# Sharing query copies between two engines and pairing score groups in a sparse attention with an expert layer on one core

## The chip, the core and the metric

The kernel runs on one core of a Trainium2 chip. The metric is the device time of one execution in microseconds (us), measured on the chip; less is better. Before the change it is 208.15 us, the median of three runs from 207.64 to 208.67. Separately, one execution was profiled. Its span, from the first instruction to the last, is 205.6 us.

## What is computed

For 4 batches, 8 heads, 768 positions and 64 elements per head, each query attends to two kinds of keys: the keys within 15 positions of its own, and 24 summary keys, each the maximum over a block of 32 keys, with the mean over the block's values. The result, 3072 rows of 512, goes through two dense layers with a gate between them.

```python
k_sum = k.reshape(B, H, nb, block, D).max(axis=3)       # block = 32, nb = 24
v_sum = v.reshape(B, H, nb, block, D).mean(axis=3)
scores_l = scale * np.matmul(q, k.transpose(0, 1, 3, 2))  # kept where |i - j| < 16
scores_s = scale * np.einsum('bhsd,bhnd->bhsn', q, k_sum) + np.log(block)
...
a = softmax of both together; x = np.matmul(a, [v, v_sum])
h = x @ w_in                                             # 512 -> 2048
g = h * (1.0 / (1.0 + np.exp(-1.702 * h)))
out = g @ w_out                                          # 2048 -> 512
```

## The kernel before, in words

**Tiles.** The 768 positions are cut in two halves of 384, the 8 heads in 4 pairs. Of a pair and a half, one *score group* (`scores`, lines 573 to 579) is 12 small matrix products (64 queries by 128 keys: own window, halo and block summaries) into one PSUM buffer of the pool `psb`, tag `big`, which has two buffers, and then one exponential on ScalarE into `a_sb`. `mask` (581 to 584) multiplies `a_sb` by a 0/1 mask on VectorE. `values` (586 to 608) multiplies two pairs' `a_sb` with the values into two banks of the pool `pmm`, tag `mm` (four buffers), and divides by the sums on VectorE (`norm`: a reciprocal and a product each). `tx` (616 to 622) transposes the result on TensorE and VectorE copies it into `xT`. `tq` (547 to 550) transposes one pair's queries on TensorE; VectorE copies them into `qT`.

**The two units.** Batch 0 is treated in two units of 384 rows each. A unit's dense layers are an input stage (`ff_in`, 640) and an output stage: 12 steps of `ff_out` (848 to 859), each with four products of 128x128 by 512, and every fourth part of a row block ended by a copy to SBUF on ScalarE (`osb`) and a write to memory from SP's queue. Attention work for what comes later is laid between these steps by a table that says after which step what is issued:

- unit 0's output stage runs `beside0` (1018 to 1031) with `plan0` (1008): the second half of batch 0. `q_late` (402 to 409) transposes a pair's late queries on TensorE into a PSUM buffer (pairs 0, 1 and 3 into `big`, pair 2 into `mm`) and an engine copies them into `qT`; then come score groups, masks, values and transposes. A `big` buffer goes from a late query to a score group when the copy has read it.
- unit 1's output stage runs `beside(1, step)` (1033 to 1051) with `plan1` (1010 to 1012): all of batch 1's attention. In the table `s02` is the score group of half 0 and pair 2, `m02` its mask, `v00` the values of half 0 and pairs 0 and 1, `x00` the transposes after it, `t2` the query transposes of pair 2, `g` the load of the gate function's table on ScalarE.

Later batches (loop at line 1100) have no halves: both are done together, with another table, `plan`, in which score groups stand in pairs.

**What sets the order.** Every engine's instructions are kept in the order in which the Python code issues them (class `_Ordered`, lines 18 to 32). A helper records them, so the profile gives line 28 for all, and its rows are told apart by tile names: `ps_q` late queries, `ps_t` other transposes, `ps_s` scores, `ps_av` values, `ps_x` transposed results, `po` output products, `ph` input products, `ps_vs` block sums of the values.

**Loads.** GpSimd's queue issues the loads of keys, values and queries (`load_batch`, 231 to 241; for batch 2 after step 2 of unit 1's output stage, line 1094). SP's queue issues the output writes, the key transposes for the next batch (`xk`, 552; after steps 9 and 11, lines 1095 and 1096), the query transposes (`xq`, 559) and the copies within the values (`value_rows`, 1053 to 1058). The block sums (`vsum`, 265 to 281) are 48 products that read a batch's values in the order of their 12 loads; for batch 2 they stand in the input stage after unit 1 (line 1124).

Of the kernel before, what the change touches and what calls it, by code (L numbers as in the profile page):

```python
# [35 lines left out]
def kernel(  # L36
# [28 lines left out]
    dve = _Ordered(tc, nc.vector)  # L65
    act = _Ordered(tc, nc.scalar)
# [187 lines left out]
    def copy(eng, out, in_):  # L254
        if eng is act:
            act.activation(out=out, in_=in_, func=ACT.Copy)
        elif eng == "dve_alone":

            dve.tensor_reduce(out=out, in_=in_.unsqueeze(len(in_.shape)), axis=AX.X, op=ALU.max)
        else:  # L260
            eng.tensor_copy(out=out, in_=in_)
# [96 lines left out]
    def turn_plain(ps, src):  # L358

        for r in range(JH):  # L360
            for h in range(2):
                pe.transpose(out=ps[h * 64:h * 64 + 64, r * 128:r * 128 + 128], in_=src[:, h, r],
                             identity=ident)
# [38 lines left out]
    def q_late(p, eng):  # L402
        if p != 2:
            ps = psb.tile([128, 2048], BF16, name="ps_q", tag="big")
        else:
            ps = pmm.tile([128, 1024], BF16, name="ps_q", tag="mm")
        turn_plain(ps[:, 0:HALF], qb2["late"][:, 2 * p:2 * p + 2])
        copy(eng, qT[p][0][:, HALF:S].rearrange("p (c r) -> p c r", r=JH),
             ps[:, 0:HALF].rearrange("p (r c) -> p c r", r=JH))
# [163 lines left out]
    def scores(b, half, p):  # L573
        a = a_sb[half, p] = attp.tile([128, 2, TH, QT], BF16, name="a_sb", tag="a_sb")
        big = psb.tile([128, 1024], F32, name="ps_s", tag="big")
        score_tiles(big, p, b % 2, half)
        act.activation(out=a.rearrange("p h t c -> p h (t c)"),
                       in_=big.rearrange("p (h c) -> p h c", h=2)[:, :, 0:HALF],
                       func=ACT.Exp, scale=scale)

    def mask(half, p):
        a = a_sb[half, p]
        dve.tensor_mul(a, a, mk[:, half * TH:(half + 1) * TH, :].unsqueeze(1)
                       .to_broadcast([128, 2, TH, QT]))

    def values(b, half, g):

        if b == 1:
            banks = [pmm.tile([128, 512], F32, name="ps_av", tag="mm") for i in range(2)]
        else:  # L590
            ps = psb.tile([128, 1024], F32, name="ps_av", tag="big")
            banks = [ps[:, i * 512:i * 512 + 512] for i in range(2)]
        pvs = []
        for i in range(2):
            p = 2 * g + i
            a = a_sb[half, p]
            pv = banks[i][:, 0:390].rearrange("p (h j c) -> p h j c", h=2, j=JH)
            pvs.append(pv)
            for hh in range(2):
                for j in range(JH):  # L600
                    for e in range(2):
                        t = 2 * j + e
                        pe.matmul(out=pv[e * 64:e * 64 + 64, hh, j, :], lhsT=a[:, hh, t, :],
                                  rhs=vw[b % 2][:, half * TH + t, p + hh * NP if b else 2 * p + hh, 0:D + 1],
                                  start=True, stop=True, skip_group_check=True)
        x2[g] = attp.tile([128, 2, JH, 2, D], F16, name="x2", tag="x2", bufs=4)
        for i in range(2):
            norm(x2[g][:, :, :, i].rearrange("p h j d -> p j h d") if b else x2[g][:, i], pvs[i])
# [7 lines left out]
    def tx(half, g):  # L616
        ps = psb.tile([128, 2, HALF], F16, name="ps_x", tag="big")
        for i in range(2):
            for j in range(JH):
                pe.transpose(out=ps[:, i, j * 128:(j + 1) * 128],  # L620
                             in_=x2[g][:, i, j].rearrange("p h d -> p (h d)"), identity=ident16)
        dve.tensor_copy(out=xTT[half][g], in_=ps)
# [243 lines left out]
    def gelu_soon():  # L866

        act.activation(out=gate[:, 1:2], in_=gate[:, 0:1], func=ACT.Gelu_apprx_sigmoid)
# [130 lines left out]
    for p in range(NP):  # L999
# [7 lines left out]

    plan0 = {1: ["q0", "q1", "q2"], 2: ["q3", "s0", "s1"], 4: ["s2", "s3"], 6: ["v0", "v1"], 8: ["x0"], 9: ["x1"]}

    plan1 = {-1: ["s00", "s01"], 1: ["t2", "m00", "m01"], 2: ["t3", "s02"], 3: ["s03", "m02"], 4: ["m03", "s10"],  # L1010
             5: ["s11", "m10"], 6: ["v00", "m11", "s12", "s13"], 7: ["v01", "g"], 8: ["m12", "m13"],
             9: ["x00", "x01", "v10"], 10: ["v11"], 11: ["x10"]}

    plan = {-1: ["s00", "s01"], 2: ["m00", "m01"], 3: ["s02", "s03"], 5: ["m02", "m03", "s10", "s11"],
# [3 lines left out]
    def beside0(slot):  # L1018
        for what in plan0.get(slot, ()):
            i = int(what[1])  # L1020
            if what[0] == "q":
                q_late(i, dve)
            elif what[0] == "s":
                scores(0, 1, i)
                mask(1, i)
                if i == NP - 1:
                    gelu_soon()
            elif what[0] == "v":
                values(0, 1, i)
            else:  # L1030
                tx(1, i)
# [37 lines left out]
    ws = keep.tile([128, 4, NT // 2, N1], F16, name="ws")  # L1069
    exp_soon()  # L1070
    beside0(-1)
    for i, (ms, part) in enumerate((ms, part) for part in range(4) for ms in range(JH)):
        ff_out(0, ms, part)
        beside0(i)
        if i in (10, 11):
            w_sum(i - 10, 0)
            w_sum(i - 10, 1)
# [22 lines left out]
    for b in range(1, B - 1):  # L1100
# [32 lines left out]
        i = 0  # L1133
# [98 lines left out]
```

## Time and profile before

| | |
|---|---|
| Median of three runs | 208.15 us (207.64 to 208.67) |
| Span of the profiled execution | 205.6 us |
| TensorE busy | 198.5 us, 2364 products |
| VectorE, ScalarE, GpSimd busy | 139.9, 123.7, 93.5 us |
| Unit 0's output stage | about 31 to 46 us of the span |
| Unit 1's output stage | about 59 to 76 us of the span |
| Moved by DMA | 27.74 MB, mean 135 GB/s |

The profiled execution has no time of its own beside its span; the three runs lie 2.0 to 3.1 us above that span. In the profile PE is TensorE's matrix products, PEld its weight loads, DVE VectorE, ACT ScalarE, POOL GpSimd and SP the queue of SyncE. A row of a timeline gives start, length, engine, operation, what is written from what, the count, and in brackets the engine's idle time before it with what ended it. A row of the chain of waits gives start, length and what the chain went through. Of a load, the profile gives the start of its issue and the time from there to its landing.

### The profile page before, as it was taken

Reading aid. Unit: us, or ns where it says so; the run is one execution under the profiler, and the core shown is the slowest. Engines: PE = TensorE matmul, PEld = TensorE weight load, DVE = VectorE, ACT = ScalarE, POOL = GpSimd, SP = SyncE. Lnnn points to the kernel's source line nnn. Section 1 sums busy time; section 2 is a strip of 40 time slices with the busy share of each in tenths; the row PEclk is TensorE's granted clock in tenths of the full one; section 3 lists DMA queues with packets and bytes.
Section 4 is the critical chain, followed back from the end, with each engine's and each line's share of the span. In section 5 each row is a group of like instructions: output and inputs, shape, how many; then the busy total and the mean of one; then the engine's idle time right before and its main releaser. Section 6 shows DMA issues by size and latency. Waiting matters only on the chain.

```text
span 205.6 us, 5854 instructions
## 1 busy us (share of the span) xinstructions
PE 198.5 (97%) x2364; PEld 138.1 (67%) x2364; DVE 139.9 (68%) x388; ACT 123.7 (60%) x237; POOL 93.5 (45%) x145
## 2 busy tenths in 40 slices
PE   7889999999999999999999999999999999999992
PEld 7658564556754566565888875566888865668882
DVE  4767795594856793898757789896769546758221
ACT  2374975728885716677772446778670577983220
POOL 7976289645899585000977036000000019990000
PEclk9999999999999999999999999999999999999999
DMA  5999999999999999999999989999023640000223
GB/s 59 153 158 198 207 212 207 204 156 233 124 145 153 177 170 135 163 145 141 139 180 158 164 162 136 130 248 154 0 105 86 149 126 3 0 0 3 102 102 105
DMA packets 97131, 27.74 MB, mean 135 GB/s; under 512 B 86720, under 2 KB 94160, under 8 KB 97104
## 3 DMA queue, kind: packets, MB, share of 16 engines
q0 software_dynamic: 71472, 13.64, 90.7%
q1 hardware_dynamic: 25632, 13.74, 32.3%
q8 instruction: 18, 0.29, 0.7%
q14 instruction: 9, 0.07, 0.1%
HBM read 27.26 MB, written 6.29 MB: 163 GB/s over the span
## 4 chain that ended last, share of the span: by engine, by line
PE 90%; DMA 4%; POOL 3%; issue 1%; DVE 1%; ACT 0%; POOLq 0%; DVEq 0%
PE ph L28 33%; PE poA L28 16%; PE po L28 11%; PE poB L28 8%; PE ps_av L28 4%; DMA v0n<-in_v_dram 4%; PE poC L28 4%; PE phA L28 4%; PE ps_s L28 3%; PE ps_t L28 1%; POOL kb L28 1%; PE ps_x L28 1%; PE phB L28 1%; PE phC L28 1%; PE phE L28 1%; PE ps_vs L28 1%
## 5 line engine op out<-in xcount | busy, mean ns | idle before, releaser
L28 PE MATMUL ph<-xT,w_in_sb 128*128 128x384 f16 x416 | 70.2, 326 | 0.1
L28 PEld LDWEIGHTS <-w_in_sb 128*128 128x128 f16 x452 | 43.7, 98 | 27.8 <-issue 0.2
L28 ACT ACTIVATE gT<-ph 128x384 f16<-128x384 f32 x104 | 49.8, 491 | 18.5 <-PE ph L28 18.2
L28 PEld LDWEIGHTS <-gT 128*128 128x128 f16 x312 | 28.8, 98 | 11.0
L28 ACT ACTIVATE a_sb<-ps_s 128x768 bf16<-128x768 f32 (+1 forms) x32 | 25.0, 826 | 12.7 <-PE ps_s L28 12.7
L28 PEld LDWEIGHTS <-gs 128*128 128x128 f16 x288 | 27.7, 98 | 3.4
L28 POOL DMA_DIRECT2D vw<-in_v_dram x36 | 24.5, 694 | 12.0 <-DMA kb<-in_k_dram 6.3
L28 POOL TENSOR_TENSOR gs<-gT 128x384 f16<-128x384 f16 x9 | 8.2, 909 | 42.4 <-ACT gT L28 42.4
L28 PE MATMUL po<-w_out_sb,gT 128*128 128x512 f16 x96 | 23.6, 380 | 0.0
L28 DVE TENSOR_TENSOR a_sb<-a_sb,mk 128x768 bf16<-128x768 bf16 x28 | 14.9, 555 | 6.5 <-ACT a_sb L28 5.9
L28 PE MATMUL poA<-ws,gs 128*128 128x256 f16 x144 | 18.7, 273 | 0.0
L28 DVE TENSOR_TENSOR x<-ps_av,rc 128x384 f16<-128x384 f32 x32 | 17.8, 558 | 1.1
L28 DVE TENSOR_TENSOR gs<-gT 128x384 f16<-128x384 f16 (+1 forms) x34 | 13.4, 393 | 7.2 <-ACT gT L28 6.9
L28 POOL DMA_DIRECT2D qb<-in_q_dram x18 | 16.6, 936 | 1.9 <-DMA w_in_sb<-in_moe_w_in_dram 1.2
L28 POOL DMA_DIRECT2D kb<-in_k_dram x16 | 15.3, 970 | 1.2 <-POOLq L1216 0.8
L28 PEld LDWEIGHTS <-kx 64*128 64x128 bf16 (+1 forms) x372 | 9.4, 95 | 6.8 <-issue 4.4
L28 DVE TENSOR_REDUCE ks<-kx 128x24 bf16<-128x768 bf16 x12 | 11.4, 948 | 3.4 <-ACT kx L28 3.2
L28 ACT ACT_TABLE_LOAD x10 | 12.8, 1283 | 1.0 <-PEq L1216 0.8
L28 ACT ACTIVATE osb<-poA 128x256 f32<-128x256 f32 x9 | 3.5, 384 | 15.8 <-PE poA L28 15.8
L28 ACT ACTIVATE s<-poA 128x256 f32<-128x256 f32 x11 | 4.2, 385 | 11.2 <-PE poA L28 11.2
L28 PEld LDWEIGHTS <-a_sb 128*64 128x64 bf16 (+2 forms) x400 | 7.8, 108 | 2.8 <-issue 1.3
L28 PE MATMUL poA<-w_out_sb,gT 128*128 128x256 f16 x72 | 9.4, 273 | 0.0
(113 smaller groups left out, 281.4 us busy)
## 6 DMA issues: line engine op xcount, KB each, us to landing
out_dram<-osb SPq DMA_DIRECT2D x23, 256.0 KB, 3.7
kb<-in_k_dram POOLq DMA_DIRECT2D x16, 192.0 KB, 6.9
qb<-in_q_dram POOLq DMA_DIRECT2D x14, 192.0 KB, 9.2
vw<-in_v_dram POOLq DMA_DIRECT2D x36, 64.0 KB, 5.7
w_out_sb<-in_moe_w_out_dram POOLq DMA_DIRECT2D x4, 512.0 KB, 13.0
w_in_sb<-in_moe_w_in_dram POOLq DMA_DIRECT2D x3, 512.0 KB, 12.7
vw<-vs SPq DMA_DIRECT2D x6, 198.0 KB, 7.1
v0n<-in_v_dram POOLq DMA_DIRECT2D x4, 192.0 KB, 7.9
```

The lines of the kernel that those rows point to most:

```text
L28: r = f(*a, **kw)
```

## The change

In `beside0`, the late query copies of pairs 1 and 3 go to ScalarE instead of VectorE. In `plan1`, half 0's score groups 2 and 3 are both issued after step 3 (before: after steps 2 and 3), half 1's groups 0 and 1 both after step 5 (before: 4 and 5), and half 1's groups 2 and 3 after step 7, behind `v01`, instead of after step 6, behind `v00`. The masks `m02` and `m10` move a step later with them. The number of instructions stays the same on TensorE, GpSimd and SP; VectorE has two fewer, ScalarE two more.

```diff
@@ plan1 @@
-    plan1 = {-1: ["s00", "s01"], 1: ["t2", "m00", "m01"], 2: ["t3", "s02"], 3: ["s03", "m02"], 4: ["m03", "s10"],
-             5: ["s11", "m10"], 6: ["v00", "m11", "s12", "s13"], 7: ["v01", "g"], 8: ["m12", "m13"],
+    plan1 = {-1: ["s00", "s01"], 1: ["t2", "m00", "m01"], 2: ["t3"], 3: ["s02", "s03"], 4: ["m02", "m03"],
+             5: ["s10", "s11"], 6: ["v00", "m10", "m11"], 7: ["v01", "s12", "s13", "g"], 8: ["m12", "m13"],
              9: ["x00", "x01", "v10"], 10: ["v11"], 11: ["x10"]}
@@ beside0 @@
             if what[0] == "q":
-                q_late(i, dve)
+                q_late(i, act if i % 2 else dve)
```

## The prediction

> **What bounds the kernel now.** I read the page first, for which engine is full and at what clock.
>
> ```profile
> span 205.6 us, 5854 instructions
> PE 198.5 (97%) x2364; PEld 138.1 (67%) x2364; DVE 139.9 (68%) x388; ACT 123.7 (60%) x237; POOL 93.5 (45%) x145
> PEclk9999999999999999999999999999999999999999
> DMA  5999999999999999999999989999023640000223
> PE 90%; DMA 4%; POOL 3%; issue 1%; DVE 1%; ACT 0%; POOLq 0%; DVEq 0%
> ```
>
> TensorE is busy for 97% of the span at the full clock, and the chain that ended last is 90% TensorE. So a change can only gain by giving TensorE fewer or cheaper instructions or by closing one of its few gaps. The DMA row is the second thing to see: 9 in nearly every slice up to two thirds of the span. Loads may be as late as TensorE is, and then TensorE time that is saved is waited away at the next load. The list of TensorE's own waits is next. This one of its rows lies in the region of the change:
>
> ```profile
> PE ps_s L28 <- DVE qT L28: 0.4, 1, 0.4
> ```
>
> The times of the runs (207.64, 208.15, 208.67) lie 2.0 to 3.1 us above the profiled span of 205.6. I work out differences within the span and add them to the median, 208.15. The three runs are 0.5% apart from end to end, and I take 0.5%, or 1.04 us, as what a measurement can tell from no change.
>
> **Edit 1: the late query copies 1 and 3 go to ScalarE.** From the timelines of the first unit's output stage and the list of groups by shape:
>
> ```profile
> 33.32 2.15 DVE L28 COPY qT<-ps_q 128x384 bf16<-128x384 bf16 x4 [1.75 <-PE ps_q L28]
> 34.51 0.36 PE L28 MATMUL ps_q<-wide,qb 128*64 128x128 bf16 x6
> 35.52 0.35 PE L28 MATMUL ps_s<-qT,kx 64*128 64x64 bf16 x12 [0.37 <-DVE qT L28]
> L28 DVE COPY qT<-ps_q x8: 548/552/558, 8.8 to 34.9; 128x384 bf16<-128x384 bf16 x8
> L28 ACT ACTIVATE xT<-ps_x 128x384 f16<-128x384 f16 x3 | 1.3, 491 | 0.5 <-PE ps_x L28 0.5
> L28 ACT ACTIVATE qT<-ps_k x3: 810/810/818, 5.9 to 12.2; 128x768 bf16<-128x768 bf16 x3
> 35.25 1.51 ACT L28 ACTIVATE a_sb<-ps_s 128x768 bf16<-128x768 f32 x2 [1.95 <-PE ps_s L28]
> ```
>
> The gap of 0.37 us stands ahead of the second score group, which takes over the PSUM buffer of query group 3 and so waits for the fourth copy. That copy could not have started much earlier on any engine: its six transposes ended at 34.51 + 0.36 = 34.87, and the copy ran from 33.32 + 2.15 - 0.55 = 34.92. Sharing the copies therefore shortens no queue that matters. It only exchanges 0.552 us on VectorE for a ScalarE copy. The trace has none of this exact copy. The same size on ScalarE is the copy of three x tiles, 491 ns: a gain of 0.06 us. The same kind of write (with a stride, into the query and key tile) at twice the size is 810 ns: a loss of 0.26, surely too far, since half of its elements are there. Those are the two ends; I take the one of the same size. Query copy 3 now stands ahead of the first exponentials on ScalarE, which begin at about 35.4 instead of 35.25 and end near 36.95; the scores that reuse their buffers come after 37.6, so that delay is covered.
>
> **Edit 2: the score groups in pairs.** The chain of waits, in order of time, in the second unit's output stage:
>
> ```profile
> 61.20 0.09 issue
> 61.29 0.49 PE ps_t L28 x6
> 61.78 0.86 PE po L28 x4
> 62.65 0.34 PE ps_t L28 x6
> 62.98 0.28 PE ps_s L28 x12
> 63.26 0.97 PE po L28 x4
> ...
> 68.48 0.46 PE ps_s L28 x24
> 68.94 0.97 PE po L28 x4
> ```
>
> Four output products after transposes take 0.86 us, after a score group 0.97. A lone group of 12 score products takes 0.28, a pair 0.46. So a lone group costs 0.28 + 0.11 = 0.39, two cost 0.78, and a pair costs 0.46 + 0.11 = 0.57. Each pairing saves 0.21 us. The change makes two pairs (steps 3 and 5) of four lone groups, and the third pair only moves from behind one block of value products to behind the next. TensorE's work falls by **0.42 us**, all of it before step 6 ends.
>
> What could take this back inside the stage? I count TensorE's new order from 62.98: products 0.86 to 63.84, pair to 64.30, products 0.97 and 0.86 to 66.13, pair to 66.59, products to 67.56, values 0.50, products to 69.03, values to 69.53, pair to 69.99, eight products to 71.82, where before they ended at 72.24.
>
> ```profile
> 63.36 0.55 DVE L28 COPY qT<-ps_t 128x768 bf16<-128x768 bf16 x1
> 68.81 1.51 ACT L28 ACTIVATE a_sb<-ps_s 128x768 bf16<-128x768 f32 x2 [0.94 <-PE ps_s L28]
> 70.20 0.60 ACT L28 ACTIVATE osb<-po 128x512 f32<-128x512 f32 x1
> ```
>
> The fourth group needs the query copy that ends at 63.91 and starts at about 64.02: covered by 0.1. ScalarE now copies the first output block (0.60, from about 63.9) and then does two exponentials (1.51) until about 65.95; the second pair takes their two buffers at 66.13 and 66.31, covered by 0.36. If it weren't, the price would be the missing part alone. The masks that move to steps 4 and 6 stay behind their exponentials, and VectorE has them done by 66.5 against 69.0. VectorE's last run of masks, copies and divisions ends where it does now, so the last block of values may find its buffer 0.1 late. Where something is late next, it is a load.
>
> **Where the gain meets the loads.** Edit 1 first. The second block of query transposes at 61.29 came 0.09 after the products ended, and it reads the last query load of the batch:
>
> ```profile
> L28 POOL DMA_DIRECT2D qb<-in_q_dram x1: 1031/1031/1031, 55.4 to 55.4; - x1
> DMA to landing us min/median/max: 5.8/5.8/5.8
> ```
>
> Landing is 55.4 + 5.8 = 61.2, just there. GpSimd issues this load, its queue does not look at TensorE's progress, and so the start at 61.29 stays where it is. The 0.06 of edit 1 is waited away; I count 0.
>
> Edit 2 next. The block sums of the next batch read its value loads, the last one in their last eight products of 48:
>
> ```profile
> L28 POOL DMA_DIRECT2D vw<-in_v_dram x1: 697/697/697, 75.2 to 75.2; - x1
> DMA to landing us min/median/max: 6.7/6.7/6.7
> 81.65 0.60 PE L28 MATMUL ps_vs<-vw,E 64*32 64x128 bf16 x48
> L28 PE MATMUL ps_vs<-vw,E x48: 213/216/227, 81.6 to 82.0; 64*32 64x128 bf16 x48
> ```
>
> The load lands at 75.2 + 6.7 = 81.9. The last of the 48 products starts at 82.0, the first of the last eight under 0.1 before. So the margin is about 0.05 us. These loads are on GpSimd's queue too, and what holds them up are the landings of earlier loads, not TensorE. If the last one lands where it did, all but 0.05 of the 0.42 us is waited at this place. A second barrier of the same kind follows: the query transposes are issued at 88.0, land 9.6 later at 97.6, and the scores that read them start at 97.89.
>
> ```profile
> L28 SPq DMA_TRANSPOSE qT<-qb x1: 4917/4917/4917, 88.0 to 88.0; - x1
> DMA to landing us min/median/max: 9.6/9.6/9.6
> 97.89 0.41 PEld L28 LDWEIGHTS <-kx 64*128 64x128 bf16 x24 [0.32 <-issue]
> ```
>
> Even a gain that survived the first would be cut to about 0.3 here unless this transfer came earlier as well. The sum: 0 - 0.42 + 0.37 = **-0.05 us**, no change that can be measured.
>
> **The rivals.** *The gain stays.* The output write and key transposes on SP's queue come earlier (next rival); if that clears them out of the loads' way, the last value load and the query transposes land earlier. Then the most is 0.42 + 0.06 = 0.48, and 207.7. For it: the transfers' total is the same. Against it: two barriers must both move.
>
> *The value loads come later* (the other sign). The output copy of the second block now has its products done at 69.03 and is not behind two late exponentials any more; it ends at about 69.7 instead of 70.8. SP's queue is in order, so its write and the key transposes behind it are issued 1.1 us earlier:
>
> ```profile
> 64.94 6.23 SPq L28 DMA_DIRECT2D out_dram<-osb  x2
> 71.34 3.22 SPq L28 DMA_TRANSPOSE kx<-kb  x2
> 76.51 0.34 SPq L28 DMA_DIRECT2D out_dram<-osb  x1
> ...
> q0 software_dynamic: 2381, 0.30, 234.1%
> q0 software_dynamic: 4735, 0.59, 174.7%
> ```
>
> The last two rows count the loads' packets from 70 to 72 and from 72 to 82 us: 1190 per us with nearly nothing of SP's in flight, 474 with it. 1.1 us more of the low rate costs the loads 1.1 x 716 = 790 packets, which take 0.7 us at the high rate and 1.7 at the low one. The last value load would land that much later, and TensorE, which is behind by 0.05 only, with it: 208.8 to 209.8. It decides as soon as that landing passes 82.0. Against it: the key transposes are over earlier too, and before the last value load the same transfers of SP's have to pass in either kernel. The Trainium skill (DMA: Bandwidth & Descriptors, Queues, rings and completion order) says that each DMA engine takes turns between the queues that have work, a packet at a time. That rule speaks for this rival and against a first-come order; the drop from 1190 to 474 agrees with it.
>
> *The pairs stall on their buffers.* If ScalarE falls behind, the second group of each pair waits for an exponential (0.75 each): up to 0.4 in two places, which eats the 0.42 but is hidden ahead of the same barrier. 208.1 to 208.5. That the change doesn't do what it says is no case: the new order on TensorE has the pairs.
>
> **How the numbers follow.** The forecast (given back at the value load, within 0.3 of no change) gets 0.55, later value loads 0.27, the gain that stays 0.15, stalled pairs 0.03. The predicted time is 208.15 - 0.05 = 208.1. Slower by over 1.04 us holds only the upper 60% of the second case, 0.16, and 0.03 for the spread of the runs: 0.19. Faster by over 1.04 us is out of reach of any case, 0.05 for the spread. Same: 0.76. The range goes from 207.4 (the gain that stays, less 0.3 of spread) to 209.4 (most of the later loads, and with them the loss end of edit 1).
>
> **What would show it.** Right: score pairs of 0.46 at steps 3 and 5; the products of step 8 ending near 71.8; a TensorE gap of 0.3 to 0.4 inside the block sums near 81.9, released by a value load; the query transposes' gap at 61.2 grown by 0.06; everything after 98 at its old place. Wrong: no gap at the block sums and all stages after them 0.4 earlier (the gain stays), or the last value load landing after 82.5 with a TensorE gap of 1 us or more (later loads). A gap on a score group that ScalarE releases would speak for the stalled pairs. A wrong count of the 0.21 per pair would show in the chain itself, as products after a pair that take more than 0.97.

## The result, and the profile after

The changed kernel takes **208.82 us** (median of 12 runs, 207.72 to 209.67) against 208.03 for the kernel before (12 runs, 207.17 to 209.12): ratio 1.0046, 95% interval 1.0026 to 1.0066. By this measurement the kernel became slower by about half a per cent. Runs over 1.5% above the fastest of their kernel are left out of the ratios here and below, which are not quotients of the medians. The means of these two sets of 12, 208.73 and 208.07, give 1.0032. A second set of 12 runs of it, told below, gave 208.16 and a ratio of 1.0011 (0.9983 to 1.0039), so the size is less sure than the first interval says. The profiled execution took 208.0 us, its span 206.3.

From the page of the changed kernel, the rows that answer those of before:

```profile
span 206.3 us, 5854 instructions
PE 198.0 (96%) x2364; PEld 138.4 (67%) x2364; DVE 138.5 (67%) x386; ACT 124.5 (60%) x239; POOL 93.8 (45%) x145
PEclk9999999999999999999999999999999999999999
DMA  5999999999999999997999989998023730000223
PE 78%; DMA 11%; DVE 4%; POOL 3%; issue 1%; ACT 1%; POOLq 0%; DVEq 0%; SPq 0%
```

TensorE is busy for 0.5 us less than before, and the span is 0.7 longer. The loss is therefore not in TensorE's work. The chain that ended last has moved from 90% TensorE to 78%, with 11% DMA and 4% VectorE (DVE): TensorE waits more. The list of its waits has two places behind the start of the kernel:

```profile
PE ps_s L28 <- DMA qT<-qb: 0.6, 1, 0.6
PE ps_s L28 <- ACT qT L28: 0.3, 1, 0.3
```

The second row is the gap at the late queries. It was 0.4 behind VectorE and is 0.3 behind ScalarE: edit 1 did what it was to do. The timeline around it shows the copies:

```profile
33.36 0.49 ACT L28 ACTIVATE qT<-ps_q 128x384 bf16<-128x384 bf16 x1 [0.24 <-PE ps_q L28]
34.73 0.49 ACT L28 ACTIVATE qT<-ps_q 128x384 bf16<-128x384 bf16 x1 [0.87 <-PE ps_q L28]
35.27 0.35 PE L28 MATMUL ps_s<-qT,kx 64*128 64x64 bf16 x12 [0.30 <-ACT qT L28]
```

A copy takes 0.49 us on ScalarE, the value taken, against 0.55 on VectorE.

**The pairs** in the chain of waits (start, length, what), in the second unit's output stage of the changed kernel:

```profile
62.15 0.34 PE ps_t L28 x6
62.48 0.86 PE po L28 x4
63.34 0.56 PE ps_s L28 x24
63.90 1.83 PE po L28 x8
65.73 0.46 PE ps_s L28 x24
66.19 0.97 PE po L28 x4
67.16 0.47 PE ps_av L28 x12
...
73.47 0.57 DVE x L28
74.04 0.04 issue
74.08 0.42 PE ps_av L28 x12
```

The pairs stand there with 0.56 (the first one waits 0.1 for its query copy) and 0.46. From the transposes at 62.15 to the first values at 67.16 the stage takes 5.01 us. But from 67.6 to 74.04 the chain runs through VectorE: divisions (`rc`, `x`), masks, copies. The last block of values waits for it. In the kernel before the same stretch is TensorE alone:

```profile
67.98 0.50 PE ps_av L28 x24
68.48 0.46 PE ps_s L28 x24
...
74.38 0.50 PE ps_av L28 x24
```

Before, it is 5.33 us from the transposes at 62.65 to the values at 67.98, and 6.90 from there to 74.88, the end of the last value block. After, it is 5.01 and then 7.34 (67.16 to 74.50). So 0.32 us are gained by the pairs and 0.44 given back. Most of the 0.44 goes to VectorE, but 0.14 of it goes to a transfer: the first 12 value products take 0.47 us here and 0.33 with edit 2 alone (below). Behind the first of them TensorE waits for the second of the two copies of the block sums into the values:

```profile
L28 SPq DMA_DIRECT2D vw<-vs x2: 585/620/654, 60.2 to 60.9; - x2
DMA to landing us min/median/max: 4.8/5.5/6.3
```

The second copy, issued at 60.9, lands at 60.9 + 6.3 = 67.2 (67.13 in the records). The last value load, which the prediction had named, was early. The last two issues of these loads, and the block sums:

```profile
L28 POOL DMA_DIRECT2D vw<-in_v_dram x2: 709/714/719, 73.3 to 74.0; - x2
DMA to landing us min/median/max: 6.3/6.3/6.3
L28 PE MATMUL ps_vs<-vw,E x48: 213/216/227, 81.3 to 81.7; 64*32 64x128 bf16 x48
```

The landing of the very last isn't in the records; with the 6.3 us of the one ahead of it, I estimate it at 74.0 + 6.3 = 80.3, 1.6 us ahead of its place before. TensorE waited for nothing from 81.3 to 81.7.

**The scores of the last batch** did wait, for the query transposes. The chain there:

```profile
120.15 3.91 PE ph L28 x24
...
126.03 8.70 DMA out_dram<-osb
...
134.81 7.25 DMA qT<-qb
142.05 0.14 issue
142.19 0.53 PE ps_s L28 x24
```

The query transposes on SP's queue wait for the landing of an output write, 8.70 us after its issue. They land at 142.05, and TensorE starts 0.6 late. In the kernel before they are issued at 135.05 and TensorE doesn't wait for them.

**The balance.** The start of the same TensorE product in both records shows how the two executions drift apart. The changed kernel is 0.18 us ahead at 21 us, after the first loads; 0.25 after the late queries, where edit 1's gain is; 0.50 after the second block of query transposes, since only the kernel before waited there for its query load; 0.81 at the first values and 0.37 after the last ones. After the scores of the last batch it is 0.30 behind, and it stays so up to TensorE's end.

**The end of the kernel.** The last output write, first in the kernel before, then after (the view of that tile, in the window that holds this one issue):

```profile
L28 SPq DMA_DIRECT2D out_dram<-osb x1: 332/332/332, 202.4 to 202.4; - x1
DMA to landing us min/median/max: 1.7/1.7/1.7
```

```profile
L28 SPq DMA_DIRECT2D out_dram<-osb x1: 332/332/332, 202.7 to 202.7; - x1
DMA to landing us min/median/max: 2.1/2.1/2.1
```

It is issued 0.30 us later and lands 0.35 us later still after that (1.71 and 2.06 in the trace's records, which are finer than the view). Nothing in the change is near this write. What lies beside it is in the view of the DMA queues, before from 201.3 to 202.1 us and after from 202.4 to 203.7:

```profile
q14 instruction: 1, 0.01, 2.4%
```

```profile
q14 instruction: 1, 0.01, 2.7%
```

Queue 14, "instruction", carries one packet (0.01 MB; 8 KB in the records) in each of the two windows: a piece of an engine's program, loaded while the kernel runs. In the records it starts 0.95 us after the issue of the third-last output write before, and 1.49 us after it in the changed kernel, where it meets the packets of the second-last write. The throughput of the DMA engines in 40 slices from 203.5 to 204.5 us, before and after, shows what follows:

```profile
GB/s 451 205 451 205 370 123 123 41 41 0 0 0 0 0 0 0 0 0 0 0 0 0 0 0 0 0 0 0 0 0 0 0 0 0 0 0 0 0 0 0
```

```profile
GB/s 82 164 246 246 205 451 164 451 492 287 451 246 532 123 492 246 205 164 123 83 41 41 0 41 0 41 0 41 41 0 41 0 0 0 0 0 0 0 0 0
```

Before, all engines end nearly together. After, from slice 20 on there are single packets of 41 GB/s with gaps between them, up to 204.27: one engine is left behind with its share of both writes, and the last write is over when that one is.

### The profile page after: what moved, and what is told of

It is laid out like the page before. It is cut to its first block, busy times and chain, and to the rows that moved or that the text cites. A ratio compares the mean times of both kernels' runs of the same rounds, so it can differ in the third digit from the quotient of the medians.

```text
span 206.3 us, 5854 instructions
## 1 busy us (share of the span) xinstructions
PE 198.0 (96%) x2364; PEld 138.4 (67%) x2364; DVE 138.5 (67%) x386; ACT 124.5 (60%) x239; POOL 93.8 (45%) x145
## 4 chain that ended last, share of the span: by engine, by line
PE 78%; DMA 11%; DVE 4%; POOL 3%; issue 1%; ACT 1%; POOLq 0%; DVEq 0%; SPq 0%
PE ph L28 25%; PE poA L28 16%; PE po L28 9%; PE poB L28 8%; DMA out_dram<-osb 4%; PE poC L28 4%; PE ps_av L28 4%; DMA v0n<-in_v_dram 4%; PE phA L28 4%; DMA qT<-qb 4%; PE ps_s L28 3%; DVE x L28 1%; POOL kb L28 1%; PE ps_t L28 1%; PE ps_x L28 1%; PE phB L28 1%
## 5 line engine op out<-in xcount | busy, mean ns | idle before, releaser
L28 ACT ACTIVATE osb<-po 128x512 f32<-128x512 f32 x6 | 3.6, 598 | 9.8 <-PE po L28 6.6
```

The source lines that it names most:

```text
L28: r = f(*a, **kw)
```

## Experiments

Three theories stood at the beginning. A: SP's queue, with the second output write and the key transposes issued earlier. B: the shorter TensorE stage meets the loads. C: ScalarE's copies. The first four runs take the change apart. Each had 12 timed runs.

**Edit 1 alone.**

```diff
-                q_late(i, dve)
+                q_late(i, act if i % 2 else dve)
```

> Edit 1 alone: late query copies 1 and 3 on ScalarE, the score groups where they were. If the loss comes from the pairs or from the moved third pair (theories A and B), this kernel is at 0 within 0.2% of the kernel before. If the loss comes from ScalarE's copies (theory C: they change when batch 1's loads and what follows run), it carries the whole loss: +0.3% to +0.6%. In the profile the gap of 0.37 us ahead of the second late score group should be about 0.3.

Measured: 208.61 us against 208.00 for the kernel before on the same chip, ratio 1.0038 (1.0005 to 1.0071). The loss is here, with no score group moved. The last write lands at +2.04 us, counted from its issue. TensorE's granted clock is 0.5 from 17.1 to 20.5 us in the profiled execution, so its span of 207.9 isn't compared. Its list of waits has the copies of the block sums again, at the first values:

```profile
PE ps_av L28 <- DMA vw<-vs: 0.6, 1, 0.6
```

**Edit 2 alone**: the whole new `plan1`, the copies on VectorE.

```diff
-    plan1 = {-1: ["s00", "s01"], 1: ["t2", "m00", "m01"], 2: ["t3", "s02"], 3: ["s03", "m02"], 4: ["m03", "s10"],
-             5: ["s11", "m10"], 6: ["v00", "m11", "s12", "s13"], 7: ["v01", "g"], 8: ["m12", "m13"],
+    plan1 = {-1: ["s00", "s01"], 1: ["t2", "m00", "m01"], 2: ["t3"], 3: ["s02", "s03"], 4: ["m02", "m03"],
+             5: ["s10", "s11"], 6: ["v00", "m10", "m11"], 7: ["v01", "s12", "s13", "g"], 8: ["m12", "m13"],
```

> Edit 2 alone: all of the new table of the second unit's output stage, the late copies on VectorE. Theories A (SP's queue: second output write and key transposes issued about 1 us earlier, and what depends on them late) and B (TensorE's shorter stage meets the loads and their order changes): +0.3% to +0.6%. Theory C (ScalarE's copies): 0 or a gain of up to 0.2%.

Measured: 207.82 against the same 208.00, ratio 0.9979 (0.9949 to 1.0008), last write at +1.72. In its chain the transposes at 62.26 are 5.02 us ahead of the values at 67.28, and the last value block ends at 74.44, 7.16 later (before 5.33 and 6.90): 0.31 gained, 0.26 given back, again behind VectorE:

```profile
62.26 0.34 PE ps_t L28 x6
...
67.28 0.33 PE ps_av L28 x12
...
73.44 0.57 DVE x L28
74.01 0.04 issue
74.06 0.38 PE ps_av L28 x12
```

**Two pairs, the third where it was**, and then **the third pair late, the others single**:

```diff
+    plan1 = {-1: ["s00", "s01"], 1: ["t2", "m00", "m01"], 2: ["t3"], 3: ["s02", "s03"], 4: ["m02", "m03"],
+             5: ["s10", "s11"], 6: ["v00", "m10", "m11", "s12", "s13"], 7: ["v01", "g"], 8: ["m12", "m13"],
```

```diff
-             5: ["s11", "m10"], 6: ["v00", "m11", "s12", "s13"], 7: ["v01", "g"], 8: ["m12", "m13"],
+             5: ["s11", "m10"], 6: ["v00", "m11"], 7: ["v01", "s12", "s13", "g"], 8: ["m12", "m13"],
```

> Only the two pairings (steps 3 and 5); the third pair stays after step 6 behind the first values, so the second block's copy on ScalarE waits behind its two exponentials as before and SP's write comes only about 0.3 us earlier. Theory A (SP's queue): 0 to -0.2%. Theory B (TensorE's 0.42 us): +0.3% to +0.6%. In the profile 0.42 us less TensorE time up to the value products of that stage in either case.

> Only the third pair moves from step 6 to step 7; the four lone groups stay alone, so TensorE has as much work as before. The second block's copy on ScalarE is ahead of the two exponentials and SP's write and key transposes come about 0.7 us earlier. Theory A (SP's queue): +0.3% to +0.6%. Theories B and C: 0 within 0.2%.

Measured: 207.77, ratio 0.9985 (0.9953 to 1.0017), and 207.72, ratio 0.9981 (0.9957 to 1.0005); the last write lands at +1.72 and +1.73. No part of edit 2 carries a loss, and theories A and B fall as its cause. What remains is edit 1, and in both kernels with edit 1 the last write is late. That gave theory D, code: the number of instructions on an engine decides when its pieces of program are loaded. The next three runs separate the copies from the counts.

**Edit 1, and two tiny clears on VectorE** in the place of the two copies:

```diff
+    tiny = consts.tile([128, 2], F32, name="tiny")
...
+                q_late(i, act if i % 2 else dve)
+                if i % 2:
+                    dve.memset(tiny[:, 0:1], 0.0)
```

> Edit 1 alone, and on VectorE two tiny clears (128x1, of a tile that nothing reads) in the place of the two copies that went to ScalarE, so that VectorE has as many instructions as before and ScalarE two more. So far edit 1 alone takes 208.6 us against 208.0, and in both kernels with edit 1 the last output write lands 2.05 us after its issue, in all others 1.72. Theory D (code): the DMA records hold pieces of 8 KB in a queue named instruction, the last but one of them at the end of the kernel; 0.6 to 0.95 us after the third-last output write is issued in the kernels without edit 1, 1.5 us after it in the two with it, where it falls on the last but one write and holds it up. What sets its place is the number of instructions. If it is VectorE's number, this kernel has the last write at 1.72 and takes 208.0 to 208.3; if it is ScalarE's, 2.05 and 208.6. Theory E (the copies themselves: ScalarE's work or the order of what waits for it): 208.6, and the last write at 2.05. Theory F (nothing but where the loads happen to land in a run): the last write at either, 208.0 to 208.6.

Measured: 208.01 against 207.90 for the kernel before on this chip, ratio 1.0013 (0.9979 to 1.0047). The copies run on ScalarE, and the last write is back at its old duration. The piece comes 0.61 us after the third-last write's issue:

```profile
L28 SPq DMA_DIRECT2D out_dram<-osb x1: 332/332/332, 202.3 to 202.3; - x1
DMA to landing us min/median/max: 1.7/1.7/1.7
```

**Before, and two idle activations on ScalarE.**

```diff
                 q_late(i, dve)
+                if i % 2:
+                    act.activation(out=tiny[:, 1:2], in_=gate[:, 0:1], func=ACT.Copy)
```

> Before, with two activations of 128x1 (copies into a tile that nothing reads) on ScalarE behind the query copies 1 and 3, which stay on VectorE: ScalarE has two instructions more, nothing else moves. Theory D, if ScalarE's number of instructions sets the place of the code piece: last output write at 2.05 us, 208.3 to 208.6. Theory D, if it is VectorE's: 1.72 and 208.0. Theory E: 208.0, since the copies are where they were. Theory F: 208.0, the last write at either.

Measured: 207.56, ratio 0.9998 (0.9976 to 1.0019), last write at +1.73. ScalarE's number does nothing to the write.

**Before, and two clears fewer on VectorE**, of columns that the next statement sets again:

```diff
         eng.memset(vw[s][96:128, 0], 0.0)
-        eng.memset(vw[s][96:128, 0, :, D:VC], 1.0)
         eng.memset(vw[s][32:64, NQ - 1], 0.0)
-        eng.memset(vw[s][32:64, NQ - 1, :, D:VC], 1.0)
+        if s == 1:
+            eng.memset(vw[s][96:128, 0, :, D:VC], 1.0)
+            eng.memset(vw[s][32:64, NQ - 1, :, D:VC], 1.0)
```

> Before, without two clears on VectorE (of the count columns of the first value tile, which the next line sets again to the same ones): VectorE has two instructions fewer, nothing else moves. Theory D, if VectorE's number sets the place of the code piece: the last output write at 2.05 us and 208.3 to 208.6, without any work on ScalarE. Theory D, if it is ScalarE's: 1.72 and 208.0. Theory E: 208.0 and 1.72. Theory F: 208.0, the last write at either.

Measured: 208.16, ratio 1.0019 (1.0000 to 1.0038). Neither the copies nor the score groups are touched, and the late write is there, at 2.04 in the records, with the piece 1.50 us after the third-last write's issue:

```profile
L28 SPq DMA_DIRECT2D out_dram<-osb x1: 332/332/332, 202.9 to 202.9; - x1
DMA to landing us min/median/max: 2.0/2.0/2.0
```

So in these kernels the lateness of the write follows VectorE's number of instructions: 386 late, 388 not. The last four runs put this to the whole change.

**The change with two clears early, with two clears late, again as it is, and edit 2 again.** The early clears stand where the two copies were; the late ones stand ahead of the last batch's products:

```diff
+    for i in range(2):
+        dve.memset(tiny[:, 0:1], 0.0)
     for i, tag in enumerate("CCEEAAA"):
```

> The whole change, and two clears of 128x1 on VectorE in the place of the two copies that left it, so that its number of instructions is that of before. The runs so far: with two instructions fewer on VectorE (the change, edit 1 alone, two clears fewer) the last output write lands 2.04 to 2.06 us after its issue and two code pieces come later (at 138.8 to 140.9 in the place of 134.8 to 136.6, and 1.5 us after the third-last output write in the place of 0.6 to 0.95); with the number of before it lands at 1.72, wherever the copies run. Theory D (VectorE's number of instructions places its code pieces, and these cost the loss): last write at 1.72, the late piece at 0.6 to 0.95, and a time with edit 2's gain in it, 207.5 to 208.1. Theory E (the change itself costs the rest, by ScalarE's copies together with the pairs): last write at 1.72, but 208.3 to 208.6, only the 0.34 of the write less than the change.

> The whole change, and the two clears on VectorE only at the beginning of the last batch's products (about 150 us), so that VectorE is two instructions short up to there and has the number of before from there on. Theory D with both pieces at work: the last write at 1.72, but the piece in the middle still at 138.8 to 140.9, among the query transposes of the last batch, and 0.1 to 0.5 us above the kernel with the early clears. Theory D with the last piece alone: 207.5 to 208.1, like the early clears. Theory E: 208.3 to 208.6 for both.

> The changed kernel itself, for the comparison with the two above on one chip and as a second look at where its loads land. Theory D and theory E: 208.5 to 208.9, the last write at 2.05. If the stall of 0.6 us at the scores of the last batch belongs to the change, it is there again; if it belonged to that one run, it is not.

> Edit 2 alone once more, as the candidate for a version that beats both kernels: 207.82 against 208.0 the first time, ratio 0.9979 with 1 inside the interval. If the pairs' 0.42 us of TensorE work are a gain that lasts: 207.4 to 207.8, 0.1 to 0.3% below before. If that was the spread of the runs: 208.0.

Measured: 207.76 with early clears (ratio 0.999, 0.9963 to 1.0017), 207.52 with late ones (0.9985, 0.9948 to 1.0022), 208.16 for the change itself (1.0011, 0.9983 to 1.0039), 207.68 for edit 2 (0.9986, 0.9956 to 1.0017); the kernel before takes 207.80 on this chip. On one chip, two clears that compute nothing make the change 0.4 to 0.6 us faster by the medians, though the intervals overlap. The last write lands at +1.73, +1.72, +2.14 and +1.73. With late clears the last piece is early again, while the piece in the middle stays where two missing instructions put it (138.6 us, with early clears 136.5); the median isn't higher for it, which speaks for the piece at the end as the one that costs. The change's own waits on TensorE in this second profile:

```profile
PE ps_t L28 <- DMA qb<-in_q_dram: 0.6, 1, 0.6
```

The wait of 0.6 at the last batch's scores is gone, and one of 0.6 at the last query load of the batch has come: which load is late differs from one execution to the next. Over all 13 profiles, by the starts of the products in the records, TensorE waits at the last batch's scores in four: the change's first (0.66), edit 1 plus two clears (0.19), late clears (0.22) and edit 2 again (0.20). It waits inside the first value block for the second copy of the block sums in five: the change's first (0.15), edit 1 alone (0.76), two pairs (0.10), two clears fewer (0.15) and early clears (0.30). Both places have kernels with 386 and with 388 instructions on VectorE, so neither wait is shown to belong to the change. All profiles together (VectorE's instructions from the page, the rest from the records):

| Kernel | VectorE's instructions | code piece after third-last write's issue, us | last write, us | from TensorE's end to the last landing, us |
|---|---|---|---|---|
| before | 388 | 0.95 | 1.71 | 2.16 |
| edit 2 alone, twice | 388 | 0.61, 0.62 | 1.72, 1.73 | 2.16, 2.17 |
| two pairs; third pair late | 388 | 0.62; 0.94 | 1.72; 1.73 | 2.16; 2.18 |
| edit 1 plus two clears | 388 | 0.61 | 1.72 | 2.17 |
| two idle activations | 388 | 0.91 | 1.73 | 2.17 |
| change plus clears, early; late | 388 | 0.61; 0.61 | 1.73; 1.72 | 2.17; 2.16 |
| **the change, twice** | 386 | 1.49, 1.50 | 2.06, 2.14 | 2.51, 2.58 |
| edit 1 alone | 386 | 1.50 | 2.04 | 2.49 |
| two clears fewer | 386 | 1.50 | 2.04 | 2.49 |

Two more figures of the records tie the write to the piece and the piece to VectorE. In the four profiles with 386 the piece takes 0.51, 0.53, 0.55 and 0.62 us, and the last write 2.04, 2.04, 2.06 and 2.14: the longer the piece, the later the write. And VectorE's own end is late with it: the DRAIN that follows its last operation starts 0.82 to 0.84 us after the third-last write's issue in these four, 0.47 in the nine with 388, though that operation starts at 0.43 in all 13.

## Why the prediction was wrong

The forecast was 208.1 and no measurable change; the first measurement is 208.82 and slower. The time lies within the range, the direction doesn't hold.

- **Edit 1, local gain of 0.06: right.** The copy takes 0.49 on ScalarE, and the gap fell from 0.37 to 0.30.
- **Edit 1, "I count 0": this is the step that failed.** The gap at 61.2 where the 0.06 was to be waited away didn't grow: it is gone in the first profile of the change and in that of edit 1 alone, and 0.6 in the second profile of the change. But the term that was missing lies elsewhere. I priced what the two copies do and where the gain is waited away, and not what their absence does to VectorE's program. Two instructions fewer move its last code piece from 0.6 to 0.95 us after the third-last output write's issue to 1.5 us after it, among the packets of the second-last write. The price is 0.3 to 0.4 us at the very end, where no work is left to cover it: no term of the sum, no rival and no wait on TensorE's list had it. It shows only as the last landing. The experiments with clears show it without the copies, and the copies without it.
- **Edit 2, 0.42 us of TensorE work: the work is right, less one wait.** Lone groups of 0.28 became pairs of 0.46; the first pair takes 0.56, since its second group waits 0.1 for the query copy that I had as covered by 0.1. What arrives at the first value block is 0.31 to 0.32.
- **"Given back at the value load": the wrong place.** In edit 2 alone 0.26 of it is given back one stage earlier, at the last value block, behind VectorE's row of masks, copies and divisions; in the change itself it is 0.44, with 0.14 for the copies of the block sums, which I had nowhere. I had seen this row ("VectorE's last run ... ends where it does now") and put 0.1 on it. The net of edit 2 alone, 0.05 gained, is by chance the sum of the prediction, and it is below what the timing can see.
- **The barriers by loads** are real, but none is fixed. The value load, which I had with a margin of 0.05, came some 1.6 us earlier in the changed kernel; a query load or the query transposes cost 0.6 in one profile and nothing in another. A margin of 0.05 read from one profile says nothing about the next run.
- **Rival "later value loads": refuted.** The output write and key transposes did come about 1.3 us earlier on SP's queue (69.99 in the place of 71.34), and the value load was earlier, not later; in none of the six profiles with the whole of edit 2 does TensorE wait at the block sums. **"The gain stays"** fell too: 0.05 of it stays. **"Stalled pairs"** is the 0.1 of the first pair, no more.

**What stays open.** The late write (0.3 to 0.4 us) less edit 2's net 0.05 explains some 0.3 us, 0.15%. This lies within the change's second interval and within those of edit 1 alone and of two clears fewer; the first measurement, with 0.26 to 0.66%, asks for more. Its 24 times as they stand ask for less: from their spread I estimate an interval of 0.05 to 0.59% around the 0.32% of their means, which has the 0.15% in it. The two waits for transfers in that profile, 0.66 and 0.15, would fill the rest, but they come in other kernels too, as counted above, and with one or two profiles per kernel I can't say whether they come more often in this one. What holds over all sets is the side: the four of kernels with 386 have ratios of 1.0011 to 1.0046, the eight with 388 have 0.9979 to 1.0013. No version here is shown to beat the kernel before: edit 2 alone (twice), its two parts and the change with clears have ratios of 0.9979 to 0.999, all six below 1, and each interval contains 1. That the late piece belongs to VectorE's program is concluded from the counts and from VectorE's late DRAIN; why two instructions fewer make it later isn't shown. The records don't name the engine that a piece is for, nor the DMA engine that it takes.

## What to carry to other kernels

When a change moves or removes a few instructions early in a kernel and the end gets later by a constant few tenths of a microsecond, look past the last engine's end: compare issue and landing of the last writes, and look for instruction packets among the DMA queues there. A dummy instruction on the engine whose count has changed tells this apart from the change itself, for the price of one run. And a gain on TensorE inside a stage is worth only what the next engine's row in that stage leaves of it: follow the chain through the stage's last dependent block before looking for loads behind it.

## What the runs showed of the hardware

Programs are loaded in pieces during the run. From the page of the changed kernel:

```profile
q8 instruction: 18, 0.29, 0.6%
q14 instruction: 9, 0.07, 0.1%
```

By the sizes in the records that is 18 pieces of 16 KB and 9 of 8 KB, 0.7% of the DMA engines' time. One of 8 KB took 0.31 to 0.62 us of an engine near the end, and one in the middle of the changed kernel took 1.19. The Trainium skill (Runtime: NRT & Kernel Launch, Instruction fetch mechanics) says that each engine's program is refilled in blocks of 16 KB by a DMA queue of its own while the block before it runs, and that a block's cost is mostly hidden. The pieces of queue 8 agree with that size, those of queue 14 are half of it; a queue for each engine can't be told from the records, which have these two. No row of TensorE's lists of waits names a piece, and what those ahead of the end cost isn't measured. At the end one piece of 8 KB is not hidden: the last write takes 0.3 to 0.4 us longer when the piece falls on the last writes, and its usual 1.71 to 1.73 us when the piece comes half a microsecond earlier.
